# Exp of two key tiles as one operation, in five of twelve attention pairs

## The chip, the cores and the metric

The kernel runs on one core of one Trainium2 chip. The metric is the device time of one execution in microseconds; for the kernel before, three runs gave 391.10, 391.92 and 392.17 us, a median of 391.92 us. Five engines work side by side: TensorE (PE: matmuls, and PEld: its weight loads), VectorE (DVE), ScalarE (ACT), GpSimd (POOL) and SyncE (SP, which here issues DMAs). Each runs its own queue in order; they wait for one another by semaphores.

## The reference

Three blocks follow each other, for two batches of 448 tokens:

```python
scores = cap * np.tanh(scale * np.matmul(q, k.transpose(0, 1, 3, 2)) / cap)   # 2 x 12 heads, 448 x 448, head size 64
attn = np.exp(scores - np.max(scores, axis=-1, keepdims=True))
attn = attn / (np.sum(attn, axis=-1, keepdims=True) + 1e-09)
x = attn @ v                                   # then as batch x 448 x 768

h = gelu_tanh(x @ w_in)                        # 768 -> 1024; u, v are its halves
v_n = (v - mean) / sqrt(var + 1e-6) * g_ln
x = x + (u * (w_sg @ v_n + b_sg)) @ w_out      # w_sg: 448 x 448 over tokens

u = x + (relu(x.T @ w_tok1) @ w_tok2).T        # token mixing
out = u + relu(u @ w_ch1) @ w_ch2              # channel mixing, 768 -> 1536 -> 768
```

## The kernel before

**Attention** goes by pairs of heads: twelve pairs, n = 0 to 5 for the first batch and 6 to 11 for the second (`attention_all`). The 448 keys of a pair are cut into three tiles of 128 (j = 0, 1, 2) and a rest of 64; the rests of two neighbouring pairs share one tile. For each tile, `scores` (L714) multiplies keys and queries on TensorE into a buffer "sc" in PSUM, of which there are two; scores are transposed, keys on the partitions, 2 heads x 448 queries along each. `weigh` then runs two operations of ACT on the tile's 896 columns: Tanh out of PSUM into a buffer of the "a" group in SBUF (L685), which frees the score buffer, and Exp in place (L694). The weights of tile j of pair n are thus a tile E[j] of shape 128 x 2 x 448, each in an "a" buffer of its own; there are 20 of these, which also hold the split weights of the feed-forward.

One step later, each E[j] is multiplied with the values on TensorE (`values` L740, the shared rest in `values_rest` L757). For the denominators, `sums` adds the tiles on DVE, E[0] + E[1] (L767), then E[2] and the rest (L1336, in `combine`), and multiplies the sum with ones on TensorE (L789). `normalise` turns the sums into reciprocals (two transposes, L806 and L811, and L808 between) and scales the product on DVE (L820); the result is split into a high and a low part (L522 on DVE or L521 on ACT for the high, L548 for the low) in a buffer of the "x" group. Of these there are six, each 128 x 2 x 896: one holds pair p of both batches.

Once the six results of a batch are there, the feed-forward's first products follow (L426), with full 128 x 128 weights. Those of the first batch are put between the calls of attention's second half. Weights come by DMA as 64-bit floats and are narrowed by ACT, DVE and POOL (lines 585 to 637). The channel mixing at the end multiplies blocks in a scheme of seven products instead of eight.

**What sets the order.** Every operation is first recorded, with a key, its engine or engines to choose from, an assumed duration, and the tiles that it reads and writes (`Plan.op`). `Plan.schedule` then builds the order for all engines: again and again it takes the operation that can start first by its own clocks, among equals the one with the lower key, and gives it a buffer of its group; an operation gets one only when enough are free for all that stand before it by key. TensorE has four tile modes (full, rows, columns and 64 x 64 quadrants, which run the calls of attention); a call of another mode than the last is charged TURN, and ranked later by STAY when the last was not a full-size one. Keys are a base (10 per pair) plus offsets from the table OFF, one letter for each kind of operation ("s": scores, "v": values, "z" and "f": sums, "n": normalise, "w": input weights, and so on). EARLY is the key at which the first batch's feed-forward joins in, KQ the place of the shared rest in its pair.

A `Part` is a view of a part of a buffer that depends on other operations as a tile of its own; its whole is allocated at the first use of any part and free after the last use of all.

Of the kernel before, what the change touches and what calls it, by code (L numbers as in the profile page):

```python
# [40 lines left out]
SPLIT = True  # L41
# [23 lines left out]
for j in range(6):  # L65
# [22 lines left out]
TURN, STAY = 200.0, 475.5  # L88
TABLE = 1290.0
COLD = 6000.0  # L90
EARLY = 76.03
KQ = 1.64
OFF = {
    "a": {
        (0, 0): -1.7, (0, 1): 5.6, (1, 1): 29.9, (1, 3): 8.0, (2, 0): 0.3, (2, 1): 4.0, (2, 2): 0.1,
        (3, 0): 22.0, (3, 1): -1.4, (3, 2): 7.3, (3, 3): 20.3,
    },
# [4 lines left out]
    },  # L102
    "f": {
        (1, 0): -3.0, (2, 0): -1.0, (3, 0): -12.5, (4, 0): 1.9, (5, 0): -1.7, (6, 0): 4.1, (8, 0): -13.6,
        (9, 0): -3.5, (10, 0): -10.3, (11, 0): -2.3,
    },
# [4 lines left out]
    },  # L111
# [4 lines left out]
    },  # L116
# [4 lines left out]
    },  # L121
    "n": {
        (1, 0): -49.3, (2, 0): 19.2, (3, 0): 1.0, (4, 0): -30.2, (5, 0): -1.3, (6, 0): 6.9, (7, 0): -4.6,
        (8, 0): -2.6, (9, 0): 2.9, (11, 0): 0.6,
    },
    "o": {
        (0, 0): -5.2, (1, 0): -12.1, (2, 0): -3.6, (3, 0): -0.9, (4, 0): 3.8, (5, 0): 18.1, (6, 0): -0.9,
        (7, 0): 1.2,
    },
# [7 lines left out]
    },  # L137
    "q": {
        (0, 0): 0.3, (0, 1): -1.0, (1, 0): 0.4, (2, 1): -3.3, (3, 0): -8.3, (3, 1): -7.6, (4, 0): -5.3,
        (4, 1): 1.6, (5, 0): 0.1, (5, 1): 1.0,  # L140
    },
# [6 lines left out]
    },  # L148
    "t": {
        (6, 1): 2.0, (6, 2): 8.4, (7, 2): 0.7, (10, 0): -4.3, (10, 1): 18.3, (10, 2): 8.5, (13, 1): 2.2,  # L150
        (13, 2): -6.2, (14, 0): 5.2, (14, 1): 17.2, (14, 2): -4.3, (16, 1): 1.2, (16, 2): 1.0,
    },
# [6 lines left out]
    },  # L159
    "w": {  # L160
        (0, 0): -6.6, (0, 1): -21.9, (1, 0): 23.9, (1, 1): -17.6, (2, 0): 1.2, (2, 1): 21.5, (3, 0): -16.4,
        (4, 0): 23.8, (4, 1): 15.4, (5, 0): -7.6, (5, 1): -0.5,
    },
    "z": {
        (0, 0): 10.3, (2, 0): -0.7, (3, 0): -2.8, (5, 0): -1.2, (6, 0): -3.7, (7, 0): 3.6, (8, 0): -0.8,
        (9, 0): -3.1, (10, 0): -2.1, (11, 0): 2.1,
# [196 lines left out]
class Net:  # L363
# [316 lines left out]
    def weigh(self, sc, nn, te, key, dt=0.2):  # L680

        nc = self.nc
        self.act(
            nn * S,
            lambda: nc.scalar.activation(te.ap, sc[:, 0:nn, :S], AF.Tanh, scale=self.qs),  # L685
            [sc, self.cb],
            [te],
            145,
            key,
            "exp",  # L690
        )
        e = self.act(
            nn * S,
            lambda: nc.scalar.activation(te.ap, te.ap, AF.Exp, scale=self.acap),  # L694
            [te, self.cb],
            [te],
            185,
            key + dt,
            "exp",
        )  # L700
        self.exps.setdefault(int(key // 10), []).append(e)

    def scores(self, qk, j, key):
# [12 lines left out]
        self.pe(3.7, fn, tiles if j else tiles[:1], [sc], key).mode = QUAD if SPLIT else ROWS  # L716
        return sc

    def scores_rest(self, qks, key):

        nc = self.nc
        sc = self.bank2()

        def fn():
            for (part, _, _), cols in zip(qks, (LO, UP)):
                for h, rows in enumerate((LO, UP)):
                    nc.tensor.matmul(sc[cols, h, :S], part(rows, KR), part(rows, QC), start=True, stop=True)

        self.pe(3.7, fn, [t for qk in qks for t in qk[1]], [sc], key).mode = QUAD
        return sc  # L730

    def values(self, qk, E, A, js, key, odd):
# [3 lines left out]
        for j in js:  # L736
# [10 lines left out]

            self.pe(3.7, av, [V, E[j]], [A], key).mode = COLS

    def values_rest(self, qks, E, As, key):  # L750
# [7 lines left out]

        self.pe(3.7, fn, [qks[0][2], qks[1][2], E], As, key).mode = QUAD

    def sums(self, E, A, key, level, odd, early, by_dma):
# [23 lines left out]
        for i, (j, e) in enumerate(tiles):  # L785
# [11 lines left out]
            self.pe(3.7, add_up, [e], [A], key).mode = COLS  # L797
# [39 lines left out]
    def attention_all(self):  # L837
        xs = []
        old = None
        for n in range(B * NP + 1):  # L840
            k0 = 10.0 * n
            odd = n % 2 == 1
            if n < B * NP:
# [5 lines left out]
                E = {j: self.a([128, 2, S]) for j in range(3)}  # L849
                E[3] = Q  # L850
                A = [As[odd], self.bank()]
                for j in range(3):
                    at = k0 + 0.4 * j + off("s", n, j)
                    sc = self.scores(qk, j, at)
                    self.weigh(sc, 2, E[j], at)
# [795 lines left out]
```

## Time and profile before

| | |
|---|---|
| runs | 391.10, 391.92, 392.17 us; median 391.92 us |
| profiled execution | 391.45 us, span 389.7 us, mean granted TensorE clock 0.998 |
| PE, PEld busy | 379.8 us (97%), 295.9 us (76%) |
| DVE, ACT, POOL busy | 313.6 us (80%), 298.0 us (76%), 92.8 us (24%) |
| Tanh (L685), Exp (L694) | 42 of each, 40.5 and 42.1 us busy |
| DMA | 77.05 MB, mean 198 GB/s |

A span runs from the first to the last instruction of the execution, and the execution's time holds what lies around it as well. Busy time counts an engine as busy from an instruction's start to its end; a matmul's end is modelled, so a busy PE may still be waiting in part. PEld rows are the loads of weights that go ahead of matmuls; where their queue waits, it says for whom.

### The profile page before, as it was taken

Reading aid. Unit: us, or ns where it says so; the run is one execution under the profiler, and the core shown is the slowest. Engines: PE = TensorE matmul, PEld = TensorE weight load, DVE = VectorE, ACT = ScalarE, POOL = GpSimd, SP = SyncE. Lnnn points to the kernel's source line nnn. Section 1 sums busy time; section 2 is a strip of 40 time slices with the busy share of each in tenths; the row PEclk is TensorE's granted clock in tenths of the full one; section 3 lists DMA queues with packets and bytes.
Section 4 is the critical chain, followed back from the end, with each engine's and each line's share of the span. In section 5 each row is a group of like instructions: output and inputs, shape, how many; then the busy total and the mean of one; then the engine's idle time right before and its main releaser. Section 6 shows DMA issues by size and latency. Waiting matters only on the chain. (4 is left out here: it accounts for less than half of the span.)

```text
span 389.7 us, 6101 instructions
## 1 busy us (share of the span) xinstructions
PE 379.8 (97%) x2050; PEld 295.9 (76%) x2050; DVE 313.6 (80%) x571; ACT 298.0 (76%) x525; POOL 92.8 (24%) x113
## 2 busy tenths in 40 slices
PE   8989999999999999999999999999999999999995
PEld 4222224746468899999999998899999999999994
DVE  0899999999788889956748999985864999876751
ACT  5999999988998688767879998866775775364720
POOL 1520321220003110000001227520230668550200
PEclk9999999999999999999999999999999999999999
DMA  7983555446445748966565899957878999992531
GB/s 242 374 339 101 176 149 203 146 146 185 149 147 187 254 145 285 308 207 208 167 220 141 247 308 264 259 148 183 228 170 199 283 209 195 220 180 43 121 112 62
DMA packets 39641, 77.05 MB, mean 198 GB/s; under 512 B 4656, under 2 KB 27568, under 8 KB 39600
## 3 DMA queue, kind: packets, MB, share of 16 engines
q1 hardware_dynamic: 30384, 63.18, 50.3%
q0 software_dynamic: 9072, 13.28, 20.2%
q8 instruction: 18, 0.29, 0.3%
q14 instruction: 23, 0.19, 0.2%
q10 hardware_dynamic: 144, 0.11, 0.1%
HBM read 50.99 MB, written 12.98 MB: 164 GB/s over the span
## 5 line engine op out<-in xcount | busy, mean ns | idle before, releaser
L1395 PE MATMUL gm<-a,a 128*128 128x448 f32 x252 | 54.6, 365 | 0.0
L1395 PEld LDWEIGHTS gm<-a,a 128*128 128x128 f32 x252 | 47.4, 188 | 3.8
L426 PE MATMUL gm<-a,a 128*128 128x448 f32 (+1 forms) x232 | 45.9, 356 | 0.0
L426 PEld LDWEIGHTS gm<-a,a 128*128 128x128 f32 x232 | 42.2, 188 | 2.0
L548 DVE TENSOR_TENSOR a<-h,a 128x384 fp32r<-128x384 f32 (+3 forms) x63 | 37.6, 603 | 5.8 <-ACT a L521 5.6
L694 ACT ACTIVATE a<-a,acap 128x896 f32<-128x896 f32 x42 | 42.1, 1049 | 0.1
L685 ACT ACTIVATE a<-sc,qs 128x896 f32<-128x896 f32 x42 | 40.5, 1009 | 1.4 <-PE sc L714 0.7
L521 ACT CAST a<-h 128x384 fp32r<-128x384 f32 (+3 forms) x56 | 29.9, 537 | 12.3 <-DVE h L1076 3.0
L585 ACT ACTIVATE r<-r 128x384 f32<-128x384 f32 (+2 forms) x64 | 36.8, 578 | 2.4 <-DMA r<-tok_in 1.0
L1282 PE MATMUL gm<-x,a 128*128 128x448 f32 x162 | 35.2, 367 | 0.8 <-DVE x L548 0.6
L1282 PEld LDWEIGHTS gm<-x,a 128*128 128x128 f32 x162 | 30.1, 188 | 4.2 <-DVE x L548 1.0
L426 PE MATMUL gm<-q,a 128*128 128x448 f32 x160 | 33.1, 365 | 0.0
L714 PE MATMUL sc<-q 64*64 64x448 f32 x264 | 30.2, 553 | 1.8 <-ACT a L685 1.8
L426 PEld LDWEIGHTS gm<-q,a 128*128 128x128 f32 x160 | 30.0, 188 | 2.3
L740 PE MATMUL gm<-a,v 128*64 128x448 f32 x144 | 31.1, 549 | 0.1
L426 PE MATMUL gm<-x,a 128*128 128x448 f32 x144 | 31.1, 369 | 0.0
L426 PEld LDWEIGHTS gm<-x,a 128*128 128x128 f32 x144 | 26.7, 188 | 5.1 <-issue 2.1
L615 DVE SCALAR_TENSOR_TENSOR t<-r,t 128x384 int32<-128x384 int32 (+2 forms) x40 | 24.3, 614 | 6.4 <-ACT t L607 6.3
L1395 PE MATMUL sc<-a,a 128*128 128x448 f32 x126 | 29.0, 366 | 0.0
L593 ACT ACTIVATE t<-r 128x384 uint16<-128x384 uint16 (+2 forms) x40 | 27.6, 694 | 1.0 <-DVE q L548 0.9
L607 ACT ACTIVATE t<-r 128x384 f16<-128x384 f32 (+2 forms) x40 | 27.4, 689 | 0.0
L426 PE MATMUL gm<-a,x 128*128 128x512 f32 x108 | 25.7, 396 | 0.8 <-DVE h L820 0.8
(154 smaller groups left out, 723.3 us busy)
## 6 DMA issues: line engine op xcount, KB each, us to landing
r<-ch_in SPq DMA_DIRECT2D x48, 384.0 KB, 3.5
r<-w_in_in SPq DMA_DIRECT2D x12, 512.0 KB, 6.1
q<-qk_in SPq DMA_DIRECT2D x11, 448.0 KB, 7.6
w<-t SPq DMA_DIRECT2D x24, 192.0 KB, 1.9
v<-va_in SPq DMA_DIRECT2D x12, 256.0 KB, 6.7
r<-w_out_in SPq DMA_DIRECT2D x6, 512.0 KB, 4.0
x<-h SPq DMA_DIRECT2D x12, 224.0 KB, 2.2
h<-x SPq DMA_DIRECT2D x12, 224.0 KB, 4.6
```

Of the source, the lines that this page charges most:

```text
L426: self.nc.tensor.matmul(view(), l, rr, start=(i + m == 0), stop=(i + m == n - 1))
L521: "ACT": ("ACT", n / 1.2 + (60 if psum else 95), lambda: nc.scalar.copy(out(), src()), False),
L548: made = {"DVE": ("DVE", n / 0.96 + 70, lambda: nc.vector.tensor_tensor(**args()), not psum)}
L585: "ACT": ("ACT", n / 1.2 + 130, lambda: nc.scalar.activation(high(), high(), AF.Copy, scale=2.0**-112), False),
L593: lambda: nc.scalar.activation(t.ap.bitcast(U16)[:, 0::2], raw.ap.rearrange("p n t -> p (n t)").bitcast(U16)[:, 1::4], AF.Copy, scale=2.0* ...
L607: lambda: nc.scalar.activation(t.ap.bitcast(F16)[:, 1::2], raw[:, :, 1].bitcast(F32), AF.Copy, scale=sign),
L685: lambda: nc.scalar.activation(te.ap, sc[:, 0:nn, :S], AF.Tanh, scale=self.qs),
L694: lambda: nc.scalar.activation(te.ap, te.ap, AF.Exp, scale=self.acap),
L714: nc.tensor.matmul(sc[at, h, :S], part(rows, ks), part(rows, QC), start=True, stop=True)
L740: nc.tensor.matmul(A[cols, :S], V[:, 2 * j + h], E[j][:, h], start=(j == 0 and not odd), stop=(j == 2 and odd),)
L1282: nc.tensor.matmul(bank.ap[:, :S], l, r, start=not more and (d, n) == (0, 0), stop=(d, n) == (2, 2), skip_group_check=more)
L1395: nc.tensor.matmul(banks[i].ap[:, :S], l, r, start=not more and (j, n) == (0, 0), stop=(j, n) == (KH - 1, 2), skip_group_check=more,)
```

## The change

In the first five pairs (TWOFOLD), E[0] and E[1] are two parts of one buffer of 128 x 4 x 448 out of the "x" group, which has the same size in bytes as a result. Each part gets its own Tanh (`squash`); after the second, one Exp (`lift`) goes over all 1,792 columns. The shared rest, E[2], and the seven other pairs keep Tanh and Exp of 896 columns each. The assumed length of an attention call on TensorE is 3.9 slots of 203 ns in place of 3.7. TURN, STAY, EARLY, KQ and nearly all offsets have other values, and a new entry "d" makes the sum of pair 8 add E[2] by an accumulating DMA of POOL (`gather`, L1197) instead of on DVE.

```diff
-TURN, STAY = 200.0, 475.5
+TURN, STAY = 105.0, 509.8
-EARLY = 76.03
-KQ = 1.64
+EARLY = 74.61
+KQ = 1.89
+TWOFOLD = range(5)
...
+    "d": {
+        (8, 0): 1.0,
+    },
...
     def weigh(self, sc, nn, te, key, dt=0.2):
-
+        self.squash(sc, nn, te, key)
+        self.lift([te], nn, te, key + dt)
+
+    def squash(self, sc, nn, te, key):
         nc = self.nc
         self.act(
             nn * S,
...
+
+    def lift(self, parts, nn, te, key):
+        nc = self.nc
         e = self.act(
             nn * S,
             lambda: nc.scalar.activation(te.ap, te.ap, AF.Exp, scale=self.acap),
-            [te, self.cb],
-            [te],
+            [*parts, self.cb],
+            parts,
             185,
-            key + dt,
+            key,
             "exp",
         )
...
-        self.pe(3.7, fn, tiles if j else tiles[:1], [sc], key).mode = QUAD if SPLIT else ROWS
+        self.pe(3.9, fn, tiles if j else tiles[:1], [sc], key).mode = QUAD if SPLIT else ROWS
...
-                E = {j: self.a([128, 2, S]) for j in range(3)}
+                two = self.buf("x", [128, 4, S]) if n in TWOFOLD else None
+                if two:
+                    E = {j: Part(two, lambda ap, j=j: ap[:, 2 * j : 2 * j + 2]) for j in range(2)}
+                else:
+                    E = {j: self.a([128, 2, S]) for j in range(2)}
+                E[2] = self.a([128, 2, S])
                 E[3] = Q
                 A = [As[odd], self.bank()]
                 for j in range(3):
                     at = k0 + 0.4 * j + off("s", n, j)
                     sc = self.scores(qk, j, at)
-                    self.weigh(sc, 2, E[j], at)
+                    if two and j < 2:
+                        self.squash(sc, 2, E[j], at)
+                        if j == 1:
+                            self.lift([E[0], E[1]], 4, two, at + 0.2)
+                    else:
+                        self.weigh(sc, 2, E[j], at)
```

## Rows read from the trace of the kernel before

**Rows 1.** The page: busy time of each engine; busy tenths in 40 slices, DVE and ACT.

```profile
PE 379.8 (97%) x2050; PEld 295.9 (76%) x2050; DVE 313.6 (80%) x571; ACT 298.0 (76%) x525; POOL 92.8 (24%) x113
...
DVE  0899999999788889956748999985864999876751
ACT  5999999988998688767879998866775775364720
```

**Rows 2.** Busy us (instructions) of each engine by stage, then clock, DMA share, GB/s.

```profile
5.70:65.60 59.90, 56.18 (x404) 15.70 (x397) 54.04 (x83) 59.66 (x69) 15.11 (x10) 1.00 0.66 233
65.60:117.50 51.90, 51.67 (x290) 31.04 (x291) 46.47 (x81) 49.07 (x75) 5.64 (x6) 1.00 0.52 162
117.50:385.60 268.10, 267.04 (x1335) 245.43 (x1334) 211.87 (x401) 187.53 (x380) 70.80 (x87) 1.00 0.77 200
```

**Rows 3.** Waits of PEld, 4 to 65.6 us: total us, times, longest us.

```profile
PEld sc L714 <- ACT a L685: 14.7, 19, 1.9
...
PEld gm L740 <- ACT a L694: 4.7, 7, 0.9
```

**Rows 4.** Waits of ACT, 5.7 to 80 us (the only one).

```profile
ACT a L685 <- PE sc L714: 0.3, 1, 0.3
```

**Rows 5.** Waits of DVE, 10.5 to 93 us (the longest is the one before 10.60).

```profile
DVE a L767 <- ACT a L694: 5.0, 1, 5.0
DVE a L548 <- POOL a L526: 0.5, 1, 0.5
```

**Rows 6.** Timeline of PE at the first full-size burst: start us, us, instruction, idle before.

```profile
65.62 4.41 PE L426 MATMUL gm<-a,x 128*128 128x512 f32 x18 [0.75 <-DVE h L820]
```

**Rows 7.** Timeline of ACT, the first pairs.

```profile
5.75 1.01 ACT L685 ACTIVATE a<-sc,qs 128x896 f32<-128x896 f32 x1 [0.32 <-PE sc L714]
6.79 1.04 ACT L694 ACTIVATE a<-a,acap 128x896 f32<-128x896 f32 x1
...
9.52 1.97 ACT L694 ACTIVATE a<-a,acap 128x896 f32<-128x896 f32 x2
11.39 1.90 ACT L685 ACTIVATE a<-sc,qs 128x896 f32<-128x896 f32 x2
13.17 1.98 ACT L694 ACTIVATE a<-a,acap 128x896 f32<-128x896 f32 x2
```

**Rows 8.** Groups of ACT by shape, whole span: busy us, mean ns, idle before.

```profile
L694 ACT ACTIVATE a<-a,acap 128x896 f32<-128x896 f32 x42 | 42.1, 1049 | 0.1
...
L593 ACT ACTIVATE t<-r 128x384 uint16<-128x384 uint16 x24 | 15.1, 637 | 0.0
...
L593 ACT ACTIVATE t<-r 128x512 uint16<-128x512 uint16 x14 | 11.1, 792 | 1.0 <-DVE q L548 0.9
...
L521 ACT CAST a<-h 128x512 fp32r<-128x512 f32 x6 | 3.7, 611 | 2.7 <-DVE h L1032 2.6
...
L1122 ACT COPY v<-h 128x64 f32<-128x64 f32 x12 | 2.9, 238 | 4.9 <-DVE h L1091 4.8
```

**Rows 9.** Timeline of DVE, up to the sums of pair 8.

```profile
10.60 1.15 DVE L767 SCALAR_TENSOR_TENSOR a<-a,guard,a 128x896 f32<-128x896 f32 x1 [4.97 <-ACT a L694]
11.66 0.42 DVE L626 TENSOR_SCALAR t<-r 128x512 int32<-128x512 int32 x1
...
20.97 0.40 DVE L522 CAST x<-h 128x448 fp32r<-128x448 f32 x1
...
35.33 1.13 DVE L767 SCALAR_TENSOR_TENSOR a<-a,guard,a 128x896 f32<-128x896 f32 x1
...
73.57 1.05 DVE L1336 TENSOR_TENSOR a<-a,a 128x896 f32<-128x896 f32 x1
```

**Rows 10.** Timeline of POOL: the first scaling of a weight.

```profile
9.70 1.69 POOL L586 TENSOR_SCALAR r<-r 128x512 f32<-128x512 f32 x1 [7.79 <-DMA r<-w_in_in]
```

**Rows 11.** DMA issues: times issued, KB each, median us to landing.

```profile
a<-a POOLq DMA_DIRECT2D x2, 192.0 KB, 6.7
```

**Rows 12.** Timeline of PE, attention calls of three lines in a row.

```profile
82.47 0.92 PE L789 MATMUL gm<-a,ones 128*64 128x448 f32 x4
83.22 0.92 PE L740 MATMUL gm<-a,v 128*64 128x448 f32 x4
84.07 0.98 PE L714 MATMUL sc<-q 64*64 64x448 f32 x8
```

More of the change, by code (lines that the diff above doesn't have):

```diff
@@ L87 @@
 LAT = {"PE": 225.0, "ACT": 160.0, "DVE": 140.0, "POOL": 140.0, "SP": 55.0}
-TURN, STAY = 200.0, 475.5
+TURN, STAY = 105.0, 509.8
 TABLE = 1290.0
 COLD = 6000.0
-EARLY = 76.03
-KQ = 1.64
+EARLY = 74.61
+KQ = 1.89
+TWOFOLD = range(5)
 OFF = {
     "a": {
-        (0, 0): -1.7, (0, 1): 5.6, (1, 1): 29.9, (1, 3): 8.0, (2, 0): 0.3, (2, 1): 4.0, (2, 2): 0.1,
-        (3, 0): 22.0, (3, 1): -1.4, (3, 2): 7.3, (3, 3): 20.3,
+        (0, 0): -4.1, (0, 1): 4.7, (0, 2): -10.4, (1, 0): 0.7, (1, 1): 29.0, (1, 2): -5.0, (1, 3): 13.7,
+        (2, 0): 1.1, (2, 1): -0.9, (2, 2): -0.2, (3, 0): 33.3, (3, 1): 1.7, (3, 2): -0.5, (3, 3): 17.5,
+    },
+    "d": {
+        (8, 0): 1.0,
@@ L97 @@
     },
     "e": {
[3 rows of a table removed]
+        (0, 0): -12.0, (1, 0): -17.2, (3, 0): -1.0, (5, 0): 13.6, (7, 0): 1.2, (8, 0): -24.2, (9, 0): 2.3,
+        (11, 0): 3.4, (12, 0): 1.1, (13, 0): 2.8, (14, 0): -24.9, (15, 0): 7.3, (16, 0): 3.2, (18, 0): -7.5,
+        (20, 0): -2.3, (21, 0): 1.4,
     },
     "f": {
-        (1, 0): -3.0, (2, 0): -1.0, (3, 0): -12.5, (4, 0): 1.9, (5, 0): -1.7, (6, 0): 4.1, (8, 0): -13.6,
-        (9, 0): -3.5, (10, 0): -10.3, (11, 0): -2.3,
+        (0, 0): -0.7, (1, 0): -5.0, (2, 0): 2.7, (3, 0): -8.8, (4, 0): 2.3, (5, 0): -0.3, (6, 0): 7.6,
@@ L106 @@
+        (8, 0): -9.9, (9, 0): -0.3, (10, 0): -13.8, (11, 0): -4.6,
     },
     "g": {
[3 rows of a table removed]
[3 rows of a table added]
     },
     "h": {
[3 rows of a table removed]
[3 rows of a table added]
     },
     "k": {
[3 rows of a table removed]
[3 rows of a table added]
     },
     "n": {
-        (1, 0): -49.3, (2, 0): 19.2, (3, 0): 1.0, (4, 0): -30.2, (5, 0): -1.3, (6, 0): 6.9, (7, 0): -4.6,
-        (8, 0): -2.6, (9, 0): 2.9, (11, 0): 0.6,
+        (0, 0): 3.5, (1, 0): -49.3, (2, 0): 12.3, (3, 0): -12.7, (4, 0): -16.8, (5, 0): -1.1, (6, 0): 5.8,
+        (7, 0): -1.5, (8, 0): -0.9, (9, 0): 8.0, (10, 0): 5.5,
     },
     "o": {
-        (0, 0): -5.2, (1, 0): -12.1, (2, 0): -3.6, (3, 0): -0.9, (4, 0): 3.8, (5, 0): 18.1, (6, 0): -0.9,
@@ L128 @@
-        (7, 0): 1.2,
+        (0, 0): 4.9, (1, 0): -15.8, (2, 0): 16.5, (3, 0): -17.4, (4, 0): 15.5, (5, 0): 22.5, (7, 0): 1.1,
     },
     "p": {
[6 rows of a table removed]
[6 rows of a table added]
     },
     "q": {
-        (0, 0): 0.3, (0, 1): -1.0, (1, 0): 0.4, (2, 1): -3.3, (3, 0): -8.3, (3, 1): -7.6, (4, 0): -5.3,
-        (4, 1): 1.6, (5, 0): 0.1, (5, 1): 1.0,
[4 rows of a table added]
     },
     "s": {
[5 rows of a table removed]
[5 rows of a table added]
     },
     "t": {
-        (6, 1): 2.0, (6, 2): 8.4, (7, 2): 0.7, (10, 0): -4.3, (10, 1): 18.3, (10, 2): 8.5, (13, 1): 2.2,
-        (13, 2): -6.2, (14, 0): 5.2, (14, 1): 17.2, (14, 2): -4.3, (16, 1): 1.2, (16, 2): 1.0,
+        (6, 2): 7.1, (7, 0): 3.4, (7, 1): -1.2, (7, 2): 0.4, (10, 0): 5.6, (10, 1): -5.0, (13, 0): 4.9,
@@ L152 @@
+        (13, 1): -5.5, (13, 2): -9.1, (14, 0): 4.9, (14, 1): -4.5, (14, 2): -2.6, (16, 1): 1.5, (16, 2): 7.3,
     },
     "v": {
[5 rows of a table removed]
[6 rows of a table added]
     },
     "w": {
-        (0, 0): -6.6, (0, 1): -21.9, (1, 0): 23.9, (1, 1): -17.6, (2, 0): 1.2, (2, 1): 21.5, (3, 0): -16.4,
-        (4, 0): 23.8, (4, 1): 15.4, (5, 0): -7.6, (5, 1): -0.5,
+        (0, 0): -9.2, (0, 1): -28.5, (1, 0): 28.8, (1, 1): -24.1, (2, 0): -3.0, (2, 1): 18.7, (3, 0): -16.0,
+        (4, 0): 26.5, (4, 1): 16.4, (5, 1): 0.2,
     },
     "z": {
-        (0, 0): 10.3, (2, 0): -0.7, (3, 0): -2.8, (5, 0): -1.2, (6, 0): -3.7, (7, 0): 3.6, (8, 0): -0.8,
@@ L166 @@
-        (9, 0): -3.1, (10, 0): -2.1, (11, 0): 2.1,
+        (0, 0): 2.1, (1, 0): -0.2, (2, 0): 2.5, (3, 0): -4.1, (4, 0): 0.5, (5, 0): 5.3, (6, 0): -6.3,
+        (7, 0): 3.6, (8, 0): -2.2, (9, 0): -6.2, (10, 0): 4.8, (11, 0): -0.7,
     },
@@ L727, in fn @@
                     nc.tensor.matmul(sc[cols, h, :S], part(rows, KR), part(rows, QC), start=True, stop=True)
-        self.pe(3.7, fn, [t for qk in qks for t in qk[1]], [sc], key).mode = QUAD
+        self.pe(3.9, fn, [t for qk in qks for t in qk[1]], [sc], key).mode = QUAD
         return sc
@@ L746, in av @@
                     )
-            self.pe(3.7, av, [V, E[j]], [A], key).mode = COLS
+            self.pe(3.9, av, [V, E[j]], [A], key).mode = COLS
     def values_rest(self, qks, E, As, key):
@@ L757, in fn @@
                     nc.tensor.matmul(As[m][cols, :S], qks[m][2][rows, 6 + h], E[rows, h], start=(m == 1), stop=(m == 0))
-        self.pe(3.7, fn, [qks[0][2], qks[1][2], E], As, key).mode = QUAD
+        self.pe(3.9, fn, [qks[0][2], qks[1][2], E], As, key).mode = QUAD
     def sums(self, E, A, key, level, odd, early, by_dma):
@@ L795, in add_up @@
                     )
-            self.pe(3.7, add_up, [e], [A], key).mode = COLS
+            self.pe(3.9, add_up, [e], [A], key).mode = COLS
     def normalise(self, n, A):
```

58 rows, old and new, of the table OFF are left out of this document.

## The prediction

> **What bounds the kernel now.** I read the busy shares by slice first, then stages, then who waits for whom, then single engines in order of time. TensorE is busy in 97% of the span [rows 1], but that hides three stages [rows 2]. From 117.5 us on, 1,335 matmuls take 267.04 us of 268.10, or 0.200 us each, with no gap to speak of: nothing that the change does to attention's ACT work can shorten this part, only let it start earlier. From 65.6 to 117.5 us TensorE is busy 51.67 of 51.90 us: attention's second half lies between bursts of the feed-forward's first products, and there is almost no hole either. The one stage with slack is 5.7 to 65.6 us, where only attention is at hand: 3.7 us of TensorE stand idle, and behind that "busy" stands a queue that waits. Its weight loads wait 14.7 us, 19 times, for a Tanh to free a score buffer, and 4.7 us for an Exp [rows 3]. ACT in turn is busy 59.66 of 59.90 us there and waits for TensorE 0.3 us in all until 80 us [rows 2, 4]. So ACT sets the pace of this stage. But DVE is as full: after its first sum at 10.60 us it waits next to nothing until 93 us [rows 5], and the first burst of full-size matmuls, at 65.62 us, is released by DVE's scaling of pair 5 (L820), 0.75 us late [rows 6].
>
> So: a saving on ACT before 65 us is worth up to its own size, if DVE lets it through; TensorE's work after it is a fixed length that moves with its start.
>
> **The change part by part.**
>
> *Exp as one.* Five pairs lose one ACTIVATE each. Two Exps of 896 columns take 1.97 us from the start of the first to the end of the second [rows 7]. The price of one of 1,792 is shown by no row, so it is worked out: an Exp of 896 takes 1.049 us on the mean, and a plain operation grows from 0.238 us at 64 columns to 0.611 us at 512, or 0.83 ns a column [rows 8], so 896 more columns add 0.746 us: 1.795 us. That is 0.175 us saved in a pair, 0.87 us in five. Bounds: if only the 128 columns between the two L593 rows (637 and 792 ns, 1.21 ns a column) told the rate, the double would take 2.13 us and lose 0.16 us a pair, 0.8 us in all; if the whole fixed part (1.049 less 0.746, 0.303 us) went, the gain is 1.5 us. I take 0.87, because the 0.83 ns rows are contiguous floats as the Exp's are, and L593's are strided. The Trainium skill ("ScalarE: Activation LUTs", What ACT_TABLE_LOAD costs) gives 280 ns plus 0.833 ns a column for an operation with a pointer operand and 93 ns of overlap back to back; by that estimate the five save 0.94 us, which no run here shows for this width yet.
>
> What lies beside it: ACT's order is already Tanh, Tanh, Exp, Exp almost everywhere [rows 7], so the merge needs no new waiting on ACT, except in pair 0, where Tanh, Exp of tile 0 come first and the second Tanh must now come before the Exp. Its scores are there by then (the second Tanh would start near 6.7 us), so ACT does not stop.
>
> *What waits longer.* The values product of tile 0 now waits for the whole double: 1.795 us from its start in place of 1.049, 0.75 us later, in five pairs. I cost it at nothing: TensorE has scores calls of the next tiles and values of the pair before to run meanwhile, and it is waiting for ACT in this stage anyway. Without that cover it is 5 x 0.75 = 3.7 us.
>
> *What comes earlier.* DVE's first sum needs tiles 0 and 1 of pair 0 and starts at 10.60 us [rows 9]. With Tanh, Tanh, double Exp from 5.75 us (Tanh starts 0.89 us apart, as the two from 11.39 us do before the Exp at 13.17) the double ends near 5.75 + 2 x 0.89 + 1.8 = 9.3 us, so the sum can start some 1.2 us earlier. Little of it lasts: DVE's next operation needs POOL's scaling, which ends at 9.70 + 1.69 = 11.39 us [rows 10], against 11.66 us now. I count 0 to 0.3 us, and take nothing on top, since it eases the same gate as the ACT saving.
>
> *The space.* The doubles take buffers of the "x" group, empty until DVE's first cast into it at 20.97 us; the sum of pair 4, nearly the last user of a double, starts at 35.33 us [rows 9]. By then two doubles and at most four results want six buffers. Cost nothing; a result that had to wait for a buffer would cost at the gate of 65.6 us one for one. Two fewer "a" buffers in each of the five pairs only give slack.
>
> *Sum of pair 8 by DMA.* The new entry "d" (8, 0) turns one DVE addition of 1.05 us (the one at 73.57 us, by its place in the order) [rows 9] into an accumulating DMA of POOL; such a DMA lands in 6.7 us [rows 11]. DVE is full there and TensorE is too, so the gain is 0 to 1.05 us and the loss, if the ones-product of pair 8 waits for the landing with nothing else ready, up to 5.6 us. That stretch holds whole bursts that need not wait, so I take 0.
>
> *The new order.* Nearly all offsets change, a turn of TensorE's tile mode is priced 105 ns in place of 200, staying 509.8 in place of 475.5, and an attention call 792 ns in place of 751. Calls of one kind follow each other in 0.75 us and across a turn in 0.85 (82.47, 83.22, 84.07) [rows 12], so the new price of a turn is nearer to what the trace has. The order can win at most the 3.7 + 0.2 us of idle TensorE [rows 2]; it can lose as much as one of the longest waits, 1.9 us [rows 3]. I take a gain of 0.6 us, about the 0.75 us with which the first burst comes late.
>
> The sum against the profiled execution's own 391.45 us (span 389.7, 1.75 us around it): less 0.87, less 0.6, is 389.98. The median of the runs lies 0.47 us above it, so I forecast 390.45, as a median 390.4 us.
>
> **The rivals.**
>
> *DVE is the real gate (391.7).* For it: DVE is as full as ACT, and the first burst waits for L820. If the gate stays at 65.6 us and attention's calls after it are only shuffled, the 0.87 us go into ACT's idle time at 80 us and later, and 0.2 us are left. Against: ACT's time freed lets it take casts of 0.4 us that DVE does now, and calls of attention done before the gate need not be done after it.
>
> *The order wins more (389.2).* If two thirds of the 3.9 us of TensorE's idle time go beside half of the saved 0.87 us: 391.92 less 2.6 less 0.4 is 388.9; with half of it, 389.5. For it: the holes are in the stage that the change touches. Against: they are waits on two full engines.
>
> *A blocked queue (slower, 393.5).* TensorE runs its queue in order. Where a values call that waits for the double stands ahead of the scores call that feeds the next Tanh, ACT itself starves for up to 0.75 us. At one pair in five this eats the gain of Exp; at two in five (1.5 us) it eats the order's 0.6 too; at four (3.0 us, less 0.87 and 0.6) the kernel is 1.5 us slower, 393.4. For it: values wait for an Exp seven times already [rows 3], at 0.7 us each. Against: the plan knows the longer Exp and can put scores first.
>
> *More turns of the mode (slower, 393.2).* A turn costs 0.1 us here [rows 12]. A plan that prices it at half may take more of them: from 15 more on it has eaten both gains, and at 28 more (some two for each of the 12 pairs) the time is 393.2. The Trainium skill ("TensorEngine Tiling (Array Packing)", its constraints) says that a change of tiling mode drains TensorE; the trace agrees in kind and prices the drain at 0.1 us.
>
> *The change does not do what it says*: a double no faster than two Exps is inside the bounds above and ends with the first rival.
>
> **How the numbers follow.** Forecast (own range 389.7 to 391.2): 0.46. DVE gate: 0.19. Order wins more: 0.14. Blocked queue: 0.14. Turns: 0.07. About 0.3% (1.2 us) is what a measurement can tell from no change: below 390.7 is faster, above 393.1 slower. Three quarters of the forecast, all of the third case and a little of the DVE gate give faster 0.51; most of the two slow cases give slower 0.18; the rest, 0.31, is the same. The range 388.5 to 393.0 leaves one in ten at either end: the large gains of a better order, and the full price of a blocked queue.
>
> **What would show it.** Right: Exps of 1,792 columns near 1.8 us, five of them; ACT reaching pair 5's first Tanh 0.9 us earlier against the same work before it; the first burst starting near 64.5 us in place of 65.62, and the batch-1 products near 116 in place of 117.5, with the 268 us behind unchanged within 0.3 us. Wrong in the ways above: the first burst still at 65.6 us behind L820; ACT waiting for scores in the first 45 us by more than 0.3 us; far more turns between matmul lines; or a double over 1.95 us. If the part after 117.5 us changes its length by more than 0.5 us, the step that takes it as fixed is the one that failed.

## The result, and the profile after

The changed kernel takes 395.77 us (median of six runs, 394.13 to 395.96) where the kernel before took 391.17 us beside it (six runs, 390.69 to 392.17). The ratio is 1.0103 [1.0091, 1.0115]: about 1%, or 4 us, slower. (The medians lie 4.6 us apart; the means of the five runs of each that were not profiled, 395.40 and 391.36 us, lie 4.0 us apart.) Forecast were 390.4 us, 388.5 to 393.0, so the time lies outside the range, on the side to which the forecast gave 0.18.

The profiled execution took 395.83 us, 4.4 us over that of before, with a span of 394.0 us. Its page first, as in [rows 1]:

```profile
PE 381.3 (97%) x2050; PEld 295.5 (75%) x2050; DVE 315.5 (80%) x578; ACT 296.3 (75%) x516; POOL 88.3 (22%) x110
...
ACT  5998997979999687777889888866874864564610
```

These totals tell next to nothing. ACT has 1.7 us less to do, about half of it by the doubles, and the first half of the span shows why that is not the time: in [rows 1] ACT's first ten slices are nearly all 9s and 8s, here there are 7s between them. The stages, cut where the first products of the second batch begin (121.70 us here, 117.5 us before), are the three lines of [rows 2]:

```profile
5.70:65.60 59.90, 55.53 (x396) 16.61 (x388) 52.79 (x84) 54.80 (x57) 6.85 (x5) 1.00 0.66 227
65.60:121.70 56.10, 53.61 (x302) 29.66 (x303) 47.88 (x82) 52.80 (x81) 7.09 (x8) 1.00 0.53 156
121.70:389.80 268.10, 267.21 (x1335) 245.46 (x1333) 213.57 (x406) 187.00 (x377) 73.09 (x87) 1.00 0.78 201
```

The last stage is the one of before: 268.10 us hold 1,335 matmuls and 267.21 us of PE, against 267.04. The whole loss is made before it, 4.2 us of it. In the first stage ACT falls from 59.66 busy us to 54.80 and PE runs 396 matmuls in place of 404; in the second PE stands 2.5 us (56.10 less 53.61) where it stood 0.2.

Who waits for whom in that time: ACT from 5.7 to 80 us (the view of [rows 4]), DVE from 10.5 to 93 us ([rows 5]), PEld from 4 to 65.6 us ([rows 3]); total us, times, longest us.

```profile
ACT x L694 <- PE sc L726: 3.9, 5, 1.7
ACT r L591 <- DMA r<-w_in_in: 2.1, 1, 2.1
...
DVE a L779 <- ACT x L706: 7.4, 3, 5.8
DVE a L1358 <- DMA a<-a: 1.9, 1, 1.9
...
PEld sc L726 <- ACT x L694: 7.9, 9, 1.2
PEld gm L752 <- ACT x L706: 5.5, 5, 1.5
PEld sc L726 <- ACT a L694: 5.5, 10, 0.7
PEld gm L752 <- ACT a L706: 4.6, 6, 1.2
```

Tanh is now L694, Exp L706, scores L726, values L752. The first of ACT's five waits for scores, 1.12 us, is the start of the kernel and no loss: it ends with the first Tanh, at 5.85 us, where before the first Tanh came at 5.75 us [rows 7]. Behind that Tanh ACT waits 2.75 us for scores (0.27, 0.60, 1.68 and 0.20), where before it waited for none, and 2.1 us for a load. Values products (L752) wait for an Exp 10.1 us in place of 4.7. DVE has a wait of 1.9 us for a DMA that it did not have. Three places follow from this.

*Place 1, scores behind values.* PE's and ACT's timelines about pairs 0 and 3 (start, us, instruction, idle before it and who ended that):

```profile
10.77 1.72 PE L752 MATMUL gm<-x,v 128*64 128x448 f32 x8 [0.69 <-ACT x L706]
...
13.18 0.98 PE L726 MATMUL sc<-q 64*64 64x448 f32 x8
...
24.70 1.78 PE L726 MATMUL sc<-q 64*64 64x448 f32 x16
...
27.17 1.72 PE L752 MATMUL gm<-x,v 128*64 128x448 f32 x8 [0.70 <-ACT x L706]
28.72 0.92 PE L752 MATMUL gm<-a,v 128*64 128x448 f32 x4
29.57 0.98 PE L726 MATMUL sc<-q 64*64 64x448 f32 x8
```

```profile
5.85 1.01 ACT L694 ACTIVATE x<-sc,qs 128x896 f32<-128x896 f32 x1 [1.12 <-PE sc L726]
...
14.23 1.01 ACT L694 ACTIVATE x<-sc,qs 128x896 f32<-128x896 f32 x1 [0.60 <-PE sc L726]
...
25.33 1.79 ACT L706 ACTIVATE x<-x,acap 128x1792 f32<-128x1792 f32 x1
27.01 1.03 ACT L706 ACTIVATE a<-a,acap 128x896 f32<-128x896 f32 x1
27.95 1.00 ACT L694 ACTIVATE x<-sc,qs 128x896 f32<-128x896 f32 x1
30.62 1.91 ACT L694 ACTIVATE x<-sc,qs 128x896 f32<-128x896 f32 x2 [1.68 <-PE sc L726]
```

Pair 0 is the plain case. The first values call on PE waits 0.69 us for the double, the scores that ACT needs next stand behind it and two calls more, at 13.18 us, and the Tanh that needs them waits 0.60 us.

About pair 3 two things come together; read them from the double at 25.33 us. The first values call needs all 1.79 us of it, and PE is idle for 0.70 us; two more values calls follow, and the scores that ACT needs next stand behind the three, at 29.57 us. ACT ends its last Tanh at 28.95 and has nothing for 1.68 us. But it is that last Tanh that frees the buffer for these scores: at the head of the queue they could have started 0.62 us sooner, and no more. The rest of the gap is the order of the Tanhs. There are two score buffers. One of them was full meanwhile: the scores of tile 1 of pair 3 were done by 26.5 us, but the order put the Tanh of tile 0 first, whose scores came at 29.57 us. So a full buffer could not be emptied while the other one was still to be filled.

*Place 2, a load.* SP issues the three loads of input weights at 58.35 us, behind a load of values and a store (SP's timeline); ACT, which scales the first of them, stops for it:

```profile
57.27 0.33 SPq L680 DMA_DIRECT2D v<-va_in  x1
57.93 0.33 SPq L847 DMA_DIRECT2D x<-h  x1
58.35 1.41 SPq L582 DMA_DIRECT2D r<-w_in_in  x3
```

```profile
61.41 1.98 ACT L706 ACTIVATE a<-a,acap 128x896 f32<-128x896 f32 x2
65.47 0.67 ACT L591 ACTIVATE r<-r 128x512 f32<-128x512 f32 x1 [2.08 <-DMA r<-w_in_in]
66.05 0.99 ACT L694 ACTIVATE a<-sc,qs 128x896 f32<-128x896 f32 x1
```

A Tanh whose scores are there stands behind the scaling in ACT's queue, and PE, which needs the score buffer that this Tanh frees, stands 1.64 us at 67.09 us. In the kernel before the same three loads went out at 54.62 us. The first burst of full-size products shows it (PE, against [rows 6]): it begins early, at 59.98 us, but with 12 matmuls alone; 24 more come at 71.16 us and the last 18 at 78.59, where before the other 36 came at 71.62 us.

```profile
59.98 3.06 PE L432 MATMUL gm<-a,x 128*128 128x512 f32 x12
67.09 0.98 PE L739 MATMUL sc<-q 64*64 64x448 f32 x8 [1.64 <-ACT a L694]
71.16 5.84 PE L432 MATMUL gm<-a,x 128*128 128x512 f32 x24
```

*Place 3, the sum by DMA.* POOL issues the accumulating DMA of pair 8 at 75.50 us; DVE needs it at 81.05 and waits for it until 82.97 us. PE then waits 0.83 us for a copy that DVE makes behind it (POOL, DVE, PE; then the DMA's row as in [rows 11]):

```profile
75.50 1.25 POOL L1219 DMA_DIRECT2D a<-a  x1 [1.25 <-DMA r<-w_in_in]
82.97 1.09 DVE L1358 TENSOR_TENSOR a<-a,a 64x896 f32<-64x896 f32 x1 [1.92 <-DMA a<-a]
85.91 2.48 PE L752 MATMUL gm<-a,v 128*64 128x448 f32 x12 [0.83 <-DVE a L528]
```

```profile
a<-a POOLq DMA_DIRECT2D x1, 448.0 KB, 7.4
```

The 6.7 us of [rows 11], from which the forecast worked, belong to transfers of 192 KB; this one has 448 KB.

### The profile page after: what moved, and what is told of

Read it like the earlier page. It is cut to its first block, busy times and chain, and to the rows that moved or that the text cites. A ratio compares the mean times of both kernels' runs of the same rounds, so it can differ in the third digit from the quotient of the medians.

```text
span 394.0 us, 6088 instructions
## 1 busy us (share of the span) xinstructions
PE 381.3 (97%) x2050; PEld 295.5 (75%) x2050; DVE 315.5 (80%) x578; ACT 296.3 (75%) x516; POOL 88.3 (22%) x110
## 5 line engine op out<-in xcount | busy, mean ns | idle before, releaser
L591 ACT ACTIVATE r<-r 128x384 f32<-128x384 f32 (+2 forms) x65 | 37.6, 583 | 4.0 <-DMA r<-w_in_in 2.1
L527 ACT CAST a<-h 128x384 fp32r<-128x384 f32 (+3 forms) x54 | 28.7, 541 | 13.7 <-PE gm L1417 3.7
L706 ACT ACTIVATE a<-a,acap 128x896 f32<-128x896 f32 x32 | 32.3, 1043 | 0.1
L694 ACT ACTIVATE a<-sc,qs 128x896 f32<-128x896 f32 x32 | 31.1, 1005 | 1.3 <-PE gm L801 0.7
L592 POOL TENSOR_SCALAR r<-r 128x512 f32<-128x512 f32 (+1 forms) x5 | 8.5, 1706 | 101.9 <-DMA w<-t 64.3
L726 PE MATMUL sc<-q 64*64 64x448 f32 x264 | 30.1, 552 | 1.0 <-ACT x L694 1.0
L1358 DVE TENSOR_TENSOR a<-a,a 64x896 f32<-64x896 f32 (+1 forms) x23 | 25.2, 1095 | 2.9 <-DMA a<-a 1.9
```

The costliest lines, as they stand in the source:

```text
L527: "ACT": ("ACT", n / 1.2 + (60 if psum else 95), lambda: nc.scalar.copy(out(), src()), False),
L591: "ACT": ("ACT", n / 1.2 + 130, lambda: nc.scalar.activation(high(), high(), AF.Copy, scale=2.0**-112), False),
L726: nc.tensor.matmul(sc[at, h, :S], part(rows, ks), part(rows, QC), start=True, stop=True)
L1358: self.dve(n, lambda: nc.vector.tensor_tensor(out=out(), in0=a(), in1=b(), op=op), r, w, key=key, port=True)
```

## The experiments

All were timed beside the kernel before on the same chip, whose medians there lie between 391.2 and 391.6 us. Beside the ratio I give, from each trace, when the second batch's first products begin on PE (a burst of 54 matmuls), since what follows has nearly one length: from there to the span's end it is 271.9 to 272.8 us in every trace but e4's (275.8):

| | median us | ratio to before | burst of 54 at us |
|---|---|---|---|
| before | 391.17 | 1 | 117.51 |
| after | 395.77 | 1.0103 [1.0091, 1.0115] | 121.70 |
| e1_merge_only | 393.28 | 1.0052 [1.0038, 1.0066] | 118.59 |
| e5_merge_1to4 | 391.50 | 1.0005 [0.9995, 1.0015] | 116.97 |
| e4_alone | 397.07 | 1.0147 [1.0125, 1.0169] | 119.22 |
| e2_split | 394.06 | 1.0069 [1.0055, 1.0083] | 121.11 |
| e9_split0 | 395.65 | 1.0097 [1.0073, 1.0121] | 121.90 |
| e3_sum_on_dve | 394.21 | 1.0072 [1.0059, 1.0086] | 121.06 |
| e6_loads | 394.24 | 1.0077 [1.0063, 1.0091] | 119.53 |
| e7_scores | 393.62 | 1.0056 [1.0037, 1.0076] | 120.50 |
| e8_mended | 392.57 | 1.0037 [1.0023, 1.0050] | 118.23 |
| e10_mended2 | 392.66 | 1.0036 [1.0025, 1.0047] | 118.17 |
| e13_split_sum_loads | 393.22 | 1.0040 [1.0025, 1.0056] | 118.89 |
| e14_mended_split | 393.27 | 1.0046 [1.0031, 1.0060] | 118.63 |
| e11_scale_first | 391.27 | 0.9998 [0.9985, 1.0011] | 116.52 |
| e12_merge_and_scale | 391.51 | 1.0002 [0.9992, 1.0013] | 117.19 |

The burst is read from one execution, which can lie some 0.5 to 1 us from its kernel's median, and ACT's first Tanh begins anywhere from 5.14 to 5.85 us in these traces; where burst and ratio differ, the ratio decides. In the diffs `ahead(x, y)` puts operation x in front of y in the finished order; nothing else of the order moves.

### The merge without the new order: e1_merge_only, e5_merge_1to4

e1 keeps the order of before. Of each pair's two Exps the earlier is dropped, the later becomes one over both tiles, and calls that need the earlier tile move behind it:

```diff
+(e1 if late is e0 else e0).fn = lambda: None
+late.fn = lambda p0=p0: self.nc.scalar.activation(self.whole[p0], self.whole[p0], AF.Exp, scale=self.acap)
...
+i = order.index(late) + 1
+order[i:i] = moved
```

> The kernel before with its own order of every queue, offsets and prices; only the Exps of tiles 0 and 1 of the first five pairs are merged, in the place of the later of the two, and the values calls that need the earlier tile follow it. Theory A (the merge is worth what it saves on ScalarE, and the new order loses the time): five times 0.18 us less on ScalarE, so 0.4 to 0.9 us faster than before, 390.3 to 390.8 us. Theory B (a double that makes values wait is what costs, in any order): slower than before by 1 us or more, 392.2 us and up.

1.0052: this merge loses 2 us. The trace shows the place, PE and ACT at pair 0:

```profile
10.62 0.97 PE L791 MATMUL gm<-x,v 128*64 128x448 f32 x4 [1.90 <-ACT x L463]
11.53 0.98 PE L765 MATMUL sc<-q 64*64 64x448 f32 x8
12.44 0.97 PE L791 MATMUL gm<-x,v 128*64 128x448 f32 x4
```

```profile
13.46 1.01 ACT L735 ACTIVATE x<-sc,qs 128x896 f32<-128x896 f32 x1 [1.06 <-PE gm L791]
```

The values product of tile 0 waits 1.90 us for the double, the next scores stand behind it, and ACT starves 1.06 us. But the scores are done at 12.51 us, 0.11 us after ACT's last Tanh ended at 12.40. What the row names as the end of the wait is a values product, the one that ends at 13.41 us: e1 puts the doubles of pairs 0 and 1 into the same buffer of the "x" group, so pair 1's first Tanh may not write before pair 0's tile 1 has been read. So some 0.9 of the 1.06 us are the price of e1's choice of buffer, not of the merge. e5 leaves pair 0 as it was, which takes both away, the queue that waits and the shared buffer:

```diff
-if n < 5 and j < 2:
+if 0 < n < 5 and j < 2:
```

> As e1_merge_only, but pair 0 keeps its two Exps; pairs 1 to 4 are merged in the order of the kernel before. Theory C (a double costs only where TensorE's queue has its values call ahead of the scores that ScalarE needs next, which in e1 was pair 0, where TensorE stood 1.9 us and ScalarE then 1.06 us): no slower than before, 390.6 to 391.5 us. Theory B (each double costs by itself): three quarters or more of e1's loss stay, 392.5 to 393.3 us.

1.0005, with 12 runs: the loss arose at pair 0. How much of it was the queue and how much the shared buffer stays open; no run gave pair 1 a buffer of its own. The four other doubles neither cost nor gain. They save 4 x 0.18 us of ACT, and ACT's timeline shows where that goes, into two waits that the kernel before did not have:

```profile
21.29 1.01 ACT L735 ACTIVATE x<-sc,qs 128x896 f32<-128x896 f32 x1 [0.35 <-PE sc L765]
...
30.64 1.01 ACT L735 ACTIVATE x<-sc,qs 128x896 f32<-128x896 f32 x1 [0.32 <-PE sc L765]
```

ACT runs ahead by 0.7 us and waits 0.67 us for scores. It comes to its next work, the scaling of a weight, 33.34 us after its first Tanh (at 38.69 us), before 33.18 (at 38.93): nothing of the saving is left by then. The burst of 54 comes 0.54 us earlier in this trace, but its first Tanh already began 0.40 us earlier. The first burst waits as in [rows 6], for the same scaling by DVE:

```profile
65.15 4.42 PE L427 MATMUL gm<-a,x 128*128 128x512 f32 x18 [0.75 <-DVE h L871]
```

That is the gate of the first rival, but the saved time was gone before it.

### The doubles in the new order: e2_split, e9_split0

e2 leaves the new order and buffers and writes each double as two Exps on the spot:

```diff
-lambda: nc.scalar.activation(te.ap, te.ap, AF.Exp, scale=self.acap),
+lambda: [nc.scalar.activation(p.ap, p.ap, AF.Exp, scale=self.acap) for p in parts],
```

> The changed kernel with every queue's order as it is; each of the five doubles is issued as two Exps of 896 columns, tile 0 first, at the same place. Theory A: nothing is won back, ScalarE does five times 0.18 us more, 395.6 to 396.7 us. Theory B: values of tile 0 can start 0.75 us sooner five times, so 1 us or more comes back, 394.8 us or less.

1.0069, so 0.34% of the 1.03% comes back although ACT has five operations more. Behind the first Tanh ACT's waits for scores fall from 2.75 us to 1.50: the 0.60 us of pair 0 are gone, and of the 1.68 us 1.10 are left:

```profile
29.64 1.91 ACT L694 ACTIVATE x<-sc,qs 128x896 f32<-128x896 f32 x2 [1.10 <-PE sc L726]
```

PE waits for no Exp there any more, and the scores start at 28.59 us, as soon as the Tanh before them ends (28.54). So of the 1.68 us some 0.6 were the double's and 1.1 are the order's. The doubles of pairs 0 and 2 cost ACT 1.2 us of waiting, where all five save 0.9: here a double costs more by making tile 0 wait than it saves. e9 splits pair 0's alone:

```diff
-lambda: nc.scalar.activation(te.ap, te.ap, AF.Exp, scale=self.acap),
+lambda: [
+    nc.scalar.activation(p.ap, p.ap, AF.Exp, scale=self.acap) for p in (parts if key < 0 else [te])
+],
```

> The changed kernel with every queue's order as it is; the double of pair 0 alone is issued as two Exps, the four others stay. Theory C (the doubles' own price is paid where nothing else is left for TensorE, in pair 0): most of what e2 won by splitting all five (0.34% of the kernel) comes back, 0.2 to 0.4% faster than the changed kernel, a ratio to before of 1.006 to 1.008. Rival (each of the five pays a part): a fifth of it, 1.009 to 1.010.

1.0097, not to be told from the changed kernel. The 0.60 us that pair 0's double costs ACT are 0.15%, less than the error of this run (0.24%), so e9 does not decide between the doubles; no run split pair 2's alone.

### The three places: e7_scores, e6_loads, e3_sum_on_dve, and all three

e7 mends place 1. Two scores calls go ahead of values calls (pair 0 and pair 3), and the Tanh whose scores are done goes first:

```diff
+at[78].new, at[76].new = at[76].new, []   # the buffer is given out at the first of the two Tanhs
+ahead(78, 84)    # Tanh of tile 1 of pair 3
+ahead(75, 85)    # scores of tile 0 of pair 3, ahead of values of pair 2
+ahead(76, 86)    # Tanh of tile 0
+ahead(79, 105)   # double of pair 3, ahead of pair 4's Tanh
+ahead(23, 33)    # scores of tile 0 of pair 1, ahead of values of tile 2 of pair 0
```

> The changed kernel with its order edited in pairs 0 and 3 alone: the scores that ScalarE starves for go ahead of a values call twice, and in pair 3 the Tanh of tile 1, whose scores hold one of two score buffers from 24.7 us on, goes ahead of that of tile 0. Theory C (the starved ScalarE, 1.68 and 0.60 us, is part of the loss): 0.4 to 1.5 us faster than the changed kernel, 394.3 to 395.4 us. Rival (VectorE, as full, is the gate): 395.5 to 396.2 us.

1.0056: 0.47% comes back. PE still waits the same 0.70 us for the double, but with ACT fed, whose gap goes from 1.68 us to 0.20 (all waits for scores behind the first Tanh from 2.75 to 0.85). What the scores put ahead and the Tanhs turned round bring each by itself was not tried:

```profile
26.71 1.72 PE L767 MATMUL gm<-x,v 128*64 128x448 f32 x8 [0.70 <-ACT x L721]
28.53 0.98 PE L741 MATMUL sc<-q 64*64 64x448 f32 x8
```

```profile
27.48 1.90 ACT L709 ACTIVATE x<-sc,qs 128x896 f32<-128x896 f32 x2
29.58 1.01 ACT L709 ACTIVATE x<-sc,qs 128x896 f32<-128x896 f32 x1 [0.20 <-PE sc L741]
```

e6 mends place 2, three loads on SP's queue and nothing else:

```diff
+for seq in (369, 376, 390):   # loads of the first input weights
+    ahead(seq, 262)           # load of values, pair 11; the store follows it
```

> The changed kernel with one edit to its order: the first three loads of the second half of w_in are issued ahead of the load and the store that stand before them on SyncE's queue. Theory A (ScalarE's 2.08 us wait for the first of them at 63 us, with the next Tanh behind it in the queue, is on the path): 0.4 to 1.2 us faster than the changed kernel's 395.8 us, 394.6 to 395.4 us. Rival (another wait takes its place): 395.5 to 396.2 us.

1.0077: 0.26% comes back. The loads go out at 50.96 us and ACT goes from Exp to scaling without a stop:

```profile
61.19 1.97 ACT L717 ACTIVATE a<-a,acap 128x896 f32<-128x896 f32 x2
63.06 0.68 ACT L602 ACTIVATE r<-r 128x512 f32<-128x512 f32 x1
```

e3 mends place 3; the sum is on DVE again:

```diff
+self.none.fn = lambda: None                 # the accumulating DMA
+rest.fn = lambda: (add(), second())         # add: F + E[2] on DVE, ahead of the rest's
```

> The changed kernel with every queue's order as it is; the sum of pair 8 adds E[2] on VectorE just ahead of its next addition, and the accumulating DMA is not issued. Theory A (VectorE's 1.92 us wait for that DMA at 81 us and the 0.83 us of TensorE behind it are on the path): 0.8 to 1.7 us faster than the changed kernel, 394.1 to 395.0 us. Rival (the later bursts would have waited anyway): within 0.4 us of it, 395.4 to 396.2 us.

1.0072: 0.31% comes back. DVE's wait is gone, PE still stands 0.77 us at 85.28 us (0.83 before), and in the place of the 1.92 us of waiting stands the addition itself, 1.39 us. So the trace shows some 0.6 us, half of what the ratio says:

```profile
80.92 1.39 DVE L810 TENSOR_TENSOR a<-a,a 128x896 f32<-128x896 f32 x1
82.34 1.08 DVE L1373 TENSOR_TENSOR a<-a,a 64x896 f32<-64x896 f32 x1
```

e8 has all three edits:

> The edits of e3, e6 and e7 together in the changed kernel, doubles kept. Theory A with C (three separate losses, each on the path): their gains add up, 3 to 4 us faster than the changed kernel, 391.8 to 392.8 us. Rival (they share one path): no faster than the best of them by more than 0.5 us, 393.5 us and up.

1.0037: 0.66% is back, where the three by themselves brought 0.26 + 0.31 + 0.47 = 1.04. Each of these gains has an error of about 0.2%, and the 0.38% between sum and whole is no larger than its own error, about 0.4%; e8's 392.57 us lies in the range that was expected if they add up. So these runs do not show whether the three overlap. In the trace the burst of 54 is 0.72 us late in place of 4.19, and the two stages are almost those of [rows 2] again (PE 55.69 and 51.55 busy us, ACT 58.61):

```profile
5.70:65.60 59.90, 55.69 (x402) 17.45 (x400) 54.08 (x88) 58.61 (x62) 8.65 (x6) 1.00 0.68 235
65.60:118.00 52.40, 51.55 (x291) 28.79 (x288) 47.68 (x79) 49.16 (x75) 4.35 (x6) 1.00 0.48 149
```

### What is left of the loss: e10_mended2, e13_split_sum_loads, e14_mended_split

e10 adds to e8 the split of pair 0 and one more scores call ahead of a values call:

```diff
+ahead(238, 244)   # scores of tile 1 of pair 9, ahead of values of tile 0 of pair 8
```

> e8_mended with two edits more: pair 0 issues two Exps in place of its double, and one scores call of pair 9 goes ahead of the values call at which TensorE stood 0.83 us. Theory C with A: 0.8 to 1.4 us faster than e8, a ratio to before of 1.000 to 1.002, so the loss is accounted for. Rival (some loss of the new order is still unnamed): 1.003 or more.

1.0036 after 1.0037: nothing. Two runs then asked whether the rest belongs to the doubles or to the order. e14 is e8 with every double split as in e2, e13 is e2, e3 and e6 together, without e7's edit:

> e8_mended with every double issued as two Exps in its place. If the rest of 0.36% hangs on the doubles: 1.000 to 1.002, faster than e8 by 0.15% or more. If it belongs to the new order: the same as e8 or slower by up to the 0.9 us that ScalarE does more, 1.0035 to 1.006.

> The changed kernel with the edits of e2, e3 and e6 together: five pairs of single Exps in the place of the doubles, the sum of pair 8 on VectorE, the three loads ahead; no scores call moved. If the doubles pay by values calls that keep TensorE's queue from the next scores, e2's, e3's and e6's gains (0.34, 0.31, 0.26%) add up: a ratio to before of 1.000 to 1.003. If what is left belongs to the new order itself: 1.004 or more.

e14 gives 1.0046 [1.0031, 1.0060]: without one double in it the mended order is still 0.4% slower than before, so what is left belongs to the new order. The doubles in it cost nothing any more; if anything they help by 0.1%, which lies within the error. e13, 1.0040, is no slower than e14, although ACT still stands the 1.10 us of place 1 in its trace: once the doubles are split, e7's edit brings nothing that can be told.

The changed kernel, e2 and e13, one after the other, take the loss of 1.03% apart: 0.34% for the five doubles, 0.29% for the sum by DMA and the loads, 0.40% for the rest of the order, each with an error of about 0.2%. A plan built from the new tables without any double was not tried, so this rest may lie in the tables or in how the doubles shaped the plan.

### The order's tables of before with doubles: e4_alone

The changed kernel with TURN, STAY, EARLY, KQ, the offsets and the 3.7 slots of before, and doubles in five pairs:

```diff
-TURN, STAY = 105.0, 509.8
+TURN, STAY = 200.0, 475.5
...
```

> The merge built into the planned order, with the offsets and prices of the kernel before (no new offsets, no sum by DMA). Theory A (planned this way the two tiles must be scored and squashed one after the other and their score buffers are held, so ScalarE starves for scores): slower than before by 1.5 to 4 us, 392.7 to 395.2 us, with ScalarE waiting for scores by more than 2 us before 40 us. Rival (only the new offsets lose the time): no slower than before, 390.3 to 391.4 us.

1.0147, slower than the changed kernel and above both ranges that were expected; ACT waits 1.4 us for scores, not over 2. By the burst of 54 it had lost 1.7 us; the rest goes after it, where the changed kernel loses nothing. PE's waits from 120 us on have one that is new:

```profile
PE gm L1299 <- ACT x L522: 3.3, 1, 3.3
```

So this was no test of the doubles: whoever lets an order be built anew, with one operation changed, gets another order everywhere, 100 us and more away from the change too. It also shows that with doubles the new tables are better than the old ones, by 0.4%; without doubles the order that they gave is worse (e2).

### Is DVE's scaling the gate: e11_scale_first, e12_merge_and_scale

e11 is the kernel before with the scaling and splitting of pair 5 on DVE put ahead of the first sum of pair 7 (the expectation calls it pair 8's); e12 does the same to e5:

```diff
+for seq in (182, 184, 185):   # scaling of pair 5, and its split into high and low
+    order.remove(at[seq])
+    order.insert(order.index(at[229]), at[seq])   # 229: first sum of pair 7
```

> The kernel before, no double, with one edit to VectorE's order: scaling and split of pair 5's result go ahead of the first sum of pair 8. Theory D (VectorE is the gate of the first full-size burst, which stood 0.75 us for that scaling): 0.3 to 0.8 us faster than before, a ratio of 0.998 to 0.9995. Rival (what is put off on VectorE comes back as a wait): 1.000 or more.

> e5_merge_1to4 with the edit of e11. Theory D (with VectorE's gate moved up, ScalarE's saved 0.7 us of pairs 1 to 4 get through): faster than e11 by 0.2 to 0.6 us, a ratio to before of 0.997 to 0.9985. Rival (the saved time goes into ScalarE's idle time whatever the gate): the same as e11 within 0.1%.

The wait of [rows 6] goes and the first burst starts 1.65 us earlier, 0.61 of it because e11's first Tanh begins at 5.14 us in place of 5.75:

```profile
63.97 4.43 PE L426 MATMUL gm<-a,x 128*128 128x512 f32 x18
```

Yet the times are 0.9998 and 1.0002. The 0.75 us before the first burst were not worth 0.75 us, and with them gone ACT's saving still reaches no end. The theory that this scaling alone holds back the gain has fallen; in e12's trace ACT again waits 0.6 us for scores, as in e5, so the saving never reached DVE's gate.

## Why the prediction was wrong

**What held.** The double takes 1.79 us (1.795 forecast), 0.18 us less than two Exps, and five of them stand in the trace. For this width the estimate by the Trainium skill that the prediction gave beside its own (280 ns and 0.833 ns a column, "ScalarE: Activation LUTs", What ACT_TABLE_LOAD costs) comes to 1.773 us; the trace agrees within 0.02. The stage after the second batch's first products kept its 268.1 us. The changes of tile mode up to there number 44 in the timeline against 46, so the rival on mode turns is out.

**What the two terms came to.** The sum took 0.87 us off for the merge and 0.6 us for the new order, from a base of 391.92 us, the median of three runs, where six give 391.17. In that order the five doubles cost 0.34%, 1.3 us (e2 against the changed kernel), and the order without doubles costs 0.69%, 2.7 us (e2 against before). Both terms had the wrong sign, and the order's is the larger miss.

**The step that failed in the merge's term** is the sentence "ACT's order is already Tanh, Tanh, Exp, Exp almost everywhere [rows 7], so the merge needs no new waiting on ACT, except in pair 0". The rows that it was read from name buffers, not tiles. Two Tanhs in a row there are mostly of tiles of different pairs, or of tile 2 and another tile of one: of the five pairs, pair 3 alone has the Tanhs of tiles 0 and 1 side by side (in e5, which keeps that order, from 25.70 us; pair 2's begin at 18.98 and 21.29). A double needs tiles 0 and 1 of *one* pair both squashed. Even in the order of before this cost ACT 0.67 us of waiting for scores, of the 0.72 that four doubles save (e5). In the new order, with two score buffers, ACT waits 2.75 us behind its first Tanh where it waited for none, 1.2 of it by the doubles and the rest by the order (e2). The prediction had named this sign: more than 0.3 us of it means the blocked queue. Nor did DVE's first sum come 1.2 us earlier: the double of pair 0 stands behind a third Tanh and starts at 8.93 us, and the sum starts at 10.75 us, before at 10.60.

**Values that wait longer** were costed at nothing, with 3.7 us if the cover is gone; the cover named was scores calls of the next tiles. In pair 0 of e1 and at 27.17 us of the changed kernel these stand behind the waiting call on TensorE's queue. e2 prices it in the new order: 0.34%, with 0.6 us of ACT's time in each of two pairs, where the rival of the blocked queue had up to 0.75 a pair. e1's 0.52% is no clean price, since a shared buffer is in it. The rival was right in its mechanism and put at 0.14; its ending, that the order can put scores first, is what e7 did by hand and what the order given had not done.

**The sum of pair 8** was taken as 0, with bounds of +1.05 and -5.6 us: the measured cost is 0.31%, 1.2 us (e3), of which the trace shows half, DVE's 1.92 us of waiting in the place of an addition of 1.39 us. What was to cover it, bursts that need not wait, was there for TensorE but not for DVE, whose queue stood.

**The new order** is the step that failed in the other term: a gain of 0.6 us was taken because it is about the 0.75 us with which the first burst came late, and nothing of the new order itself went into it. It cost 0.69% with no double in it (e2) and still 0.40% with the sum on DVE and the loads ahead (e13). The loads' 0.26% (e6) is a term that the prediction did not have: it counted POOL's new DMA and never asked where on SP's queue the loads of the first input weights come to stand.

**The gain of ACT** of 0.87 us: where nothing else goes wrong it is worth 0.0 ± 0.1% (e5). The first rival put this down to DVE's scaling; in e5 the saving went into waits for scores before it came to that gate, and moving the gate changed nothing (e12). Idle time before [rows 6] was taken as worth its own length; e11 shows that it was not.

**What stays open.** Of the 1.03% some 0.36% remains after all edits, and it is the new order's. No single place is shown for it. In e10's trace the values of the shared rest come at 84.80 us, against 84.87 before, so up to there the two are level (e10's first Tanh began 0.28 us earlier); the next full-size burst comes at 88.04 us, against 87.24, behind a wait for a Tanh:

```profile
87.13 0.98 PE L750 MATMUL sc<-q 64*64 64x448 f32 x8 [0.60 <-ACT a L716]
```

Whether that wait is the cause was not tried. No kernel here beats the one before.

## What to carry to other kernels

Two operations made into one save a fixed part (0.18 us here), and the price is that the first result comes as late as the second: before merging, look in the trace whether both inputs are ready at one time, tile by tile and not line by line, what stands behind the first result's reader on its queue, and who else uses the buffer that holds both. A saving on an engine that is "busy 99%" is worth nothing until the trace of the saved kernel shows a later stage starting earlier; here four doubles saved 0.7 us, the engine then waited 0.67 us for its input, and nothing could be measured. When a change comes with a new order of everything, price the order by itself (the change undone inside it, and the change alone inside the old order), and read every queue, the load queue too.

## What the runs showed of the hardware

In pair 0 of the changed kernel a wait of 0.69 us at the head of TensorE's queue became 0.60 us of idle time on ScalarE, whose next scores stood behind it and two calls more; with the wait gone (e2) the idle time was gone too. One Exp of 1,792 columns took 1.79 us, two of 896 in a row 1.97. An accumulating DMA of 448 KB that POOL issued at 75.50 us landed in 7.4 us and was waited for until 82.97 us, 7.5 us from issue to use; the addition on VectorE in its place took 1.39 us (e3). And a first burst that started 1.04 us earlier, counted from ACT's first Tanh (e11), left the time as it was: 0.9998 [0.9985, 1.0011].
